# A re-searched instruction order for linear attention with a gated feed-forward layer, with two subtractions moved to VectorE

## The chip, the cores and the metric

The kernel runs on one core of a Trainium2 chip. The metric is the device time of one execution in microseconds, the median of several runs; less is better. The core has a TensorE for matrix products, a VectorE, a ScalarE and a GpSimd for element-wise work, and SP (SyncE), whose queue issues every transfer of this kernel. Each engine works through its own list of instructions in order and waits at an instruction until the semaphores that it names have come.

## The reference

Softmax of q over the features, softmax of k over the sequence, a linear attention without a score matrix, and then a feed-forward layer whose two branches are multiplied:

```python
def _attn_ref(q, k, v):                      # each (8, 8, 576, 64)
    q_s = np.exp(q - np.max(q, axis=-1, keepdims=True))
    q_s = q_s / (np.sum(q_s, axis=-1, keepdims=True) + 1e-09)
    k_s = np.exp(k - np.max(k, axis=2, keepdims=True))
    k_s = k_s / (np.sum(k_s, axis=2, keepdims=True) + 1e-09)
    kv = np.einsum('bhsd,bhse->bhde', k_s, v)
    return np.einsum('bhsd,bhde->bhse', q_s, kv)
...
x = attn_out.transpose(0, 2, 1, 3).reshape(4608, 512)
return (x @ w_a) * (x @ w_b) @ w_out         # d_ff = 1536
```

## The kernel before

The 4,608 tokens are worked through in nine chunks of 512. For each chunk the attention gives x, and x goes through the two weight matrices and the output matrix. All large products are done at single precision by splitting each operand into a high and a low part and adding three products. From the second chunk on the two weight products are written as a seven-product block scheme (Strassen's): groups `kx`, `ky` and `ka` of twelve products of 256 columns each, into three banks; the output product is written in the same way from the fifth chunk on, in half groups of six products into the banks `po0` to `po3`. The weight operands `ws` and the right-hand operands `xo` do not all fit on the chip. They are stored to memory once (`dw`, `dr`) and loaded again and again, 512 KB and 256 KB at a time, into a few rotating buffers. A load can start only when the last product that read its buffer is done, and at most eight loads are under way. The attention for the next chunk is interleaved: `qt` are tiles of queries, of which VectorE takes the maxima (`st`), ScalarE the exponentials with their sums; `kt` and `vt` are keys and values, `pk` their products.

The first chunk is a stage of its own, in which everything is started. It works on four pairs of heads. For each pair g the class `Startup` has a small function: `mc` takes the maximum of the keys, `ek` their exponential, `tr` five transposes on TensorE (`pka`, `pkb`), `cA` and `cD` the copies back, `pk` the product with the values; `qs` takes the maxima of the queries, `qu` subtracts them, `qe` takes the exponential, `qr` its sum, `qn` the reciprocal, `qm` scales by it, `pq` transposes the queries, `qw` copies them, and `px` multiplies them with the pair's key-value product. In the version before, `qu` and `qm` are GpSimd's for all four pairs. `wu` multiplies a tile of ones with itself, nine times ahead of the first transposes and twice between the first and the second lot; nothing reads its result.

What order the engines' lists are in is not left to the code. `ORDER` at the top of the file holds, for each of the five engines, a list of positions which says in what order the instructions, counted as the code records them, are to stand; `in_order` chains them. These lists come out of a search that is not in the file.

Of the kernel before, what the change touches and what calls it, by code (L numbers as in the profile page):

```python
# [7 lines left out]
F32 = mybir.dt.float32  # L8
# [23 lines left out]
        "0-15 20 16-19 21-48 53-59 49-52 60 75-84 61-74 97-100 91-94 85-88 101-102 109-110 103-105 111 "  # L32
        "89-90 112-114 106-108 127-132 95-96 115-120 133-138 171-174 121-123 222-225 175 124-126 139-159 "
        "165 200-209 163 166 164 168 170 160-162 176-181 167 273-276 182-187 169 188-196 210 197-199 216 "
        "227-232 239-241 315-318 233-238 242-247 226 248-260 277-282 211-215 366-369 283-285 264 217-218 "
        "286-288 219-221 289-291 270-271 292-294 267 301-302 268 261 295-300 272 269 309 265 408-411 262 "
        "320-322 319 266 323-325 263 306 326-328 344-353 332-333 312 303 334 394-395 329-331 412 335-343 "
        "370-378 437-446 379-390 459-462 391-393 304 307-308 305 354 310-311 313-314 363-365 360-361 "
        "425-427 413-418 357 428-430 355-356 396 431-433 358 419-424 501-504 405 362 402-403 487-488 "
        "434-436 359 399-400 404 406-407 401 543 529-530 397-398 447 456-458 453-454 568 455 463-471 "  # L40
        "450-452 475-483 472-474 492-494 484-486 448-449 505-510 498-500 489-491 517-522 511-513 534-536 "
        "514-516 523-525 495-497 526-528 537-539 544-546 531-533 547-558 575 629-638 559-564 576-577 "
        "565-567 540-542 581-592 687 578-580 572-574 623-625 569-571 617-622 605-616 626-628 736 639-644 "
        "651-656 645-650 737 657-662 593-604 663-674 738-747 675-686 688-705 748-759 712-723 727-728 "
        "730-731 729 784 775-777 785 732-734 760-765 786 766-771 706-711 735 781-783 797-802 724-726 "
        "803-814 772-773 815-820 832-843 774 844-849 778-780 850-855 871-872 874-875 873 856-861 880-891 "
        "862-867 876 910-911 868-869 877-878 870 879 913-914 787-796 892-903 821 907-908 904-906 916-939 "
        "909 940-957 912 915 958-963 985-986 964-975 982-984 988-993 987 1021 976-977 1022 978 822-831 "
        "979-980 1000-1008 994-999 1009-1011 1018-1020 981 1012-1013 1024-1028 1014 1029 1015-1016 "
        "1042-1053 1030-1041 1072-1083 1096-1097 1023 1017 1105-1106 1099-1100 1107 1098 1101 1060-1065 "  # L50
        "1054-1056 1066-1071 1057-1059 1102-1103 1084-1095 1104 1114-1137 1141-1142 1138-1139 1144-1145 "
        "1147-1148 1146 1156-1161 1168-1179 1162-1167 1149 1108-1111 1143 1140 1112-1113 1180-1191 "
        "1228-1239 1219-1220 1216-1217 1204-1209 1218 1222-1223 1150 1225-1226 1151 1210-1215 1192-1197 "
        "1224 1221 1152-1154 1227 1240-1251 1155 1198-1203 1252-1253 1261-1263 1258-1259 1264-1269 "
        "1255-1256 1270-1275 1257 1276-1287 1254 1260 1372-1391 1288-1299 1336-1347 1312-1323 1333-1335 "
        "1300-1305 1330-1331 1348-1353 1327-1329 1354-1359 1306-1311 1369-1370 1332 1363-1365 1371 "
        "1324-1326 1360-1361 1366-1367 1392-1397 1464 1398-1403 1362 1404-1415 1368 1416-1427 1465-1470 "
        "1428-1445 1452-1453 1446-1451 1471-1476 1458-1459 1455-1456 1477-1482 1457 1483-1488 1461-1463 "
        "1498-1499 1454 1521-1532 1501-1510 1460 1533-1544 1489-1491 1545-1550 1495-1496 1492-1493 "
        "1557-1568 1551-1556 1494 1584-1586 1569-1574 1581-1582 1500 1497 1587-1589 1623-1624 1593-1599 "  # L60
        "1590-1592 1583 1600-1604 1575-1580 1617-1618 1620-1621 1605-1616 1625-1628 1622 1619 1511-1520 "
        "1629-1655 1659-1676 1656-1658 1701-1702 1698-1699 1695-1696 1704-1705 1697 1737-1738 1703 "
        "1677-1682 1706 1746-1747 1683-1694 1707-1718 1700 1740-1741 1719-1724 1742 1725-1736 1743-1744 "
        "1749-1753 1739 1745 1755-1760 1754 1761-1766 1748 1767-1778 1785-1796 1779-1781 1797-1802 "
        "1782-1783 1803-1808 1821-1822 1827-1829 1809-1820 1833-1850 1784 1824-1825 1851-1856 1826 "
        "1860-1861 1823 1857-1858 1863-1864 1830-1832 1866-1867 1859 1862 1865 1868-1910 1941-1952 "
        "1932-1933 1938-1939 1935-1936 2085-2094 1929-1930 1917-1928 1940 1934 1968-1969 1953-1964 1970 "
        "1911-1916 1977-1982 1931 1937 1983-2000 1971-1972 1974-1976 1965-1967 2013-2018 2049-2051 2001 "
        "2052 2019 2053 1973 2043-2044 2002 2020-2021 2003-2006 2022-2024 2007-2011 2040-2041 2046-2048 "
# [1676 lines left out]
```

## Time and profile before

| | us |
|---|---|
| median of three timed runs | 934.03 |
| lowest and highest of them | 933.91, 935.12 |
| the profiled execution | 938.13 |
| its span, first to last instruction | 936.4 |
| TensorE busy | 914.3 (98%) |
| VectorE busy | 714.4 (76%) |
| ScalarE busy | 492.1 (53%) |
| GpSimd busy | 113.6 (12%) |

The mean granted clock of TensorE over the span is 0.995 of full speed. 306.40 MB are moved, at a mean of 327 GB/s. Of the chain of work that ended last, 76% of the span is TensorE's, 11% transfers, 5% VectorE, 4% ScalarE. The engines overlap, so busy shares do not add up; only the idle time of the engine that sets the pace, and the clock at which it works, can be won.

### The profile page before, as it was taken

What the parts mean: (1) busy time and instruction counts of PE and PEld (TensorE: products, weight loads), DVE (VectorE), ACT (ScalarE), POOL (GpSimd) and SP (SyncE); (2) the same over time, 40 slices, a digit from 0 to 9 for tenths busy, and PEclk for the clock granted to TensorE, in tenths of its full rate; (3) what the DMA queues carried; (4) which work ended last, traced back from release to release, by engine and by line L of the source; (5) the groups of instructions that cost most, each with busy time, mean ns of one, the idle gap of its engine ahead of it and who ended that gap; (6) DMA issues with size and microseconds to landing.
All of it is one profiled execution on the core that took longest, in us unless ns stands there. A gap on an engine that the chain in (4) does not pass through costs nothing.

```text
span 936.4 us, 19574 instructions
## 1 busy us (share of the span) xinstructions
PE 914.3 (98%) x7171; PEld 855.8 (91%) x7171; DVE 714.4 (76%) x1554; ACT 492.1 (53%) x1350; POOL 113.6 (12%) x96
## 2 busy tenths in 40 slices
PE   7999999999999999999999989999999999999998
PEld 6667888898898999999999989999999999999997
DVE  5889988587877777679877777588868776776556
ACT  5988787555433446545834653336543554343322
POOL 4545344422000000000000000000000000000000
PEclk8999999999999999999999999999999999999999
DMA  9899999999999999999899888998999799959962
GB/s 356 321 380 398 367 343 359 354 346 331 348 353 321 351 347 313 376 317 377 316 344 334 315 299 293 298 378 288 356 314 392 254 348 307 391 197 321 335 245 108
DMA packets 124735, 306.40 MB, mean 327 GB/s; under 512 B 13408, under 2 KB 30432, under 8 KB 124640
## 3 DMA queue, kind: packets, MB, share of 16 engines
q1 hardware_dynamic: 124640, 305.16, 92.1%
q8 instruction: 57, 0.93, 0.4%
q14 instruction: 38, 0.31, 0.1%
HBM read 256.87 MB, written 48.23 MB: 326 GB/s over the span
## 4 chain that ended last, share of the span: by engine, by line
PE 76%; DMA 11%; DVE 5%; ACT 4%; issue 2%; SPq 1%; POOL 0%; DVEq 0%; ACTq 0%
PE kx L855 24%; PE po L1518 15%; PE ky L855 12%; PE po L884 8%; PE ka L855 6%; PE pt L830 6%; DMA ws<-dw 3%; PE px L786 2%; PE pk L604 2%; DMA kt<-in_k 2%; DMA mr<-dq 2%; DMA qt<-in_q 1%; DMA xo<-dr 1%; ACT qt L697 1%; DMA dw<-ws 1%
## 5 line engine op out<-in xcount | busy, mean ns | idle before, releaser
L855 PE MATMUL kx<-xo,ws 128*128 128x256 f32 x2304 | 316.6, 283 | 1.9 <-ACT u L1621 1.0
L855 PEld LDWEIGHTS kx<-xo,ws 128*128 128x128 f32 x2304 | 293.5, 189 | 9.3 <-ACT u L1621 2.3
L855 PE MATMUL ky<-xo,ws 128*128 128x256 f32 x1152 | 158.4, 282 | 1.2 <-DMA ws<-dw 0.8
L855 PEld LDWEIGHTS ky<-xo,ws 128*128 128x128 f32 x1152 | 146.5, 188 | 3.0 <-PE px L786 0.9
L1472 DVE TENSOR_TENSOR left<-cc,left 128x256 fp32r<-128x256 f32 x245 | 96.6, 421 | 53.3 <-ACT left L1471 52.6
L1471 ACT CAST left<-cc 128x256 fp32r<-128x256 f32 x245 | 92.4, 405 | 71.0 <-DVE cc L1487 36.5
L1518 PE MATMUL po<-xo,left 128*128 128x256 f32 x750 | 106.8, 283 | 1.9 <-DMA xo<-dr 1.9
L1518 PE MATMUL po<-kept,left 128*128 128x256 f32 x720 | 100.5, 282 | 1.6 <-DVE acc L1527 1.6
L1518 PEld LDWEIGHTS po<-xo,left 128*128 128x128 f32 x750 | 97.3, 190 | 2.9 <-issue 1.9
L1518 PEld LDWEIGHTS po<-kept,left 128*128 128x128 f32 x720 | 91.9, 189 | 1.9 <-DVE acc L1527 1.8
L855 PE MATMUL ka<-xo,ws 128*128 128x256 f32 x576 | 81.5, 283 | 2.1 <-DMA ws<-dw 2.1
L830 PE MATMUL pt<-xo,ws 128*128 128x512 f32 x288 | 77.7, 406 | 2.9 <-ACT ga L837 2.2
L697 ACT ACTIVATE qt<-qt,st 128x64 f32<-128x64 f32 x224 | 76.2, 343 | 7.5 <-DVE st L694 6.3
L855 PEld LDWEIGHTS ka<-xo,ws 128*128 128x128 f32 x576 | 74.1, 188 | 3.4 <-issue 1.7
L1621 ACT COPY u<-kx 128x512 f32<-128x512 f32 x48 | 28.2, 587 | 82.3 <-DVE cc L1615 41.2
L830 PEld LDWEIGHTS pt<-xo,ws 128*128 128x128 f32 x288 | 52.8, 189 | 18.5 <-ACT ga L837 3.1
L534 POOL PARTITION_ALL_REDUCE mx<-m x20 | 15.8, 790 | 431.9 <-DVE m L545 431.9
L1487 DVE TENSOR_TENSOR cc<-cc 128x256 f32<-128x256 f32 x140 | 56.9, 420 | 1.8
L884 PE MATMUL po<-wo_w,gh 128*128 128x512 f32 x192 | 56.4, 398 | 0.0
L1642 ACT COPY cc<-kx 128x256 f32<-128x256 f32 x48 | 17.9, 372 | 72.4 <-PE kx L855 72.4
L1602 ACT COPY u<-kx 128x512 f32<-128x512 f32 x48 | 28.1, 585 | 50.1 <-PE kx L855 50.1
L1607 ACT COPY u<-kx 128x512 f32<-128x512 f32 x48 | 28.0, 584 | 48.7 <-PE kx L855 48.3
(173 smaller groups left out, 1376.8 us busy)
## 6 DMA issues: line engine op xcount, KB each, us to landing
ws<-dw SPq DMA_DIRECT2D x277, 512.0 KB, 6.5
xo<-dr SPq DMA_DIRECT2D x125, 256.0 KB, 5.7
dw<-ws SPq DMA_DIRECT2D x42, 512.0 KB, 6.4
mr<-dq SPq DMA_DIRECT2D x112, 128.0 KB, 6.5
raw<-in_w_ab SPq DMA_DIRECT2D x24, 512.0 KB, 7.2
vt<-in_v SPq DMA_DIRECT2D x28, 325.0 KB, 6.3
qt<-in_q SPq DMA_DIRECT2D x32, 256.0 KB, 5.9
kt<-in_k SPq DMA_DIRECT2D x24, 320.0 KB, 5.2
```

The lines of the kernel that those rows point to most:

```text
L604: nc.tensor.matmul(pk[h * D:(h + 1) * D], kt[:, j, h], vt[:, j, h], start=(j == 0), stop=(j == J - 1),)
L697: nc.scalar.activation(out=qt[:, j, h], in_=qt[:, j, h], func=AF.Exp, bias=st[:, h, 0, j:j + 1], accum_out=st[:, h, 1, j:j + 1],)
L830: nc.tensor.matmul(pt, w[:, wp], x[g][:, xp], start=(g == 0 and i == 0), stop=(g == NP - 1 and i == 2),)
L855: ins = nc.tensor.matmul(pt[:, n], w[:, n, wp, c], x[:, xp, c], start=(first and n == 0 and i == 0), stop=(i == 5), skip_group_check=True,)
L884: nc.tensor.matmul(po[t], a[:, ts], wo[f][:, w], start=(f == 0 and i == 0), stop=(f == NF - 1 and i == 2),)
L1471: nc.scalar.copy(out=a[:, 0], in_=cc[:, n, part])
L1472: nc.vector.tensor_tensor(out=a[:, 1], in0=cc[:, n, part], in1=a[:, 0].bitcast(F32), op=ALU.subtract)
L1487: nc.vector.tensor_tensor(out=o, in0=x, in1=y, op=op)
L1518: nc.tensor.matmul(pt[:, t], x.left[:, ap, t * P:(t + 1) * P], w[:, wp], start=(first and t == 0 and n == 0), stop=(n == 2), skip_group_ch ...
L1602: nc.scalar.copy(out=u3, in_=kx)
L1607: nc.scalar.copy(out=u2, in_=kx)
L1621: nc.scalar.copy(out=u4, in_=kx)
```

## The change

Three things are written differently, and the lists for all five engines are new.

```diff
-    whole_q = (nc.gpsimd, nc.gpsimd, nc.gpsimd, nc.gpsimd)
-    WARM = (9, 2)
-    QM = (0, 1, 2, 3)
+    whole_q = (nc.vector, nc.vector, nc.gpsimd, nc.gpsimd)
+    QM = (1, 2, 3)
...
         def wu(n):
-            if n == 0:
-                at["wu"] = ps.tile([P, T], F32, name="wu", tag="po3")
-            for i in range(WARM[n]):
-                nc.tensor.matmul(at["wu"][:, 0:P], ones, ones, start=True, stop=True)
+            wu = ps.tile([P, T], F32, name="wu", tag="po3")
+            for w in (T, T, H):
+                nc.tensor.matmul(
+                    wu[:, 0:w].rearrange("p (n q) -> p n q", q=P), ones,
+                    ones.unsqueeze(1).broadcast_to([P, w // P, P]), start=True, stop=True,
+                )
...
-        "wu0 mc0 qs0 ek0 mc1 qu0 qe0 tr0 wu1 qs1 cD0 qu1 ek1 qr0 qn0 mc2 qe1 tr1 qm0 cA0 ek2 pk0 qr1 "
+        "wu0 mc0 qs0 ek0 mc1 qu0 qe0 tr0 qs1 cD0 qu1 ek1 qr0 qn0 mc2 qe1 tr1 qm0 cA0 ek2 pk0 qr1 "
...
 ORDER = {
     "PE": (
-        "0-15 20 16-19 21-48 53-59 49-52 60 75-84 61-74 97-100 91-94 85-88 101-102 109-110 103-105 111 "
...
+        "0-2 7 3-6 8-36 45 37-40 46 41-44 47-51 53-62 67-76 52 63-66 83-85 89-94 77-79 86 101-102 87-88 "
```

So the subtractions of the first two pairs and the scaling of the first are VectorE's, and GpSimd has three instructions fewer; the eleven products of ones of 128 columns are three of 512, 512 and 256 columns, all ahead of the first transposes. The new lists come from a search that counts a transfer as landing later than the search before did. They hold the same other instructions; line numbers above the change are one lower in the new file, and the numbers at the ends of tile names are eight lower in the late stages.

Three places show how the lists differ. The first is the start on VectorE, before and after (`mc` are maxima of keys, line 1169 the maxima of queries, 1175 the subtraction, 1192 the sum, 1195 and 1196 the reciprocal, 1199 the scaling, `pkb` what the last transpose of a pair wrote):

```order
L1132 TENSOR_REDUCE mc<-kt_first_77 128x1
L1132 TENSOR_REDUCE mc<-kt_first_79 128x1
L1169 TENSOR_REDUCE qst<-qts 128x8 x2
L1150 COPY kt_first_77<-pkb 128x128
L1169 TENSOR_REDUCE qst<-qts 128x8
L1192 TENSOR_REDUCE qst_143<-qts 128x8
L1132 TENSOR_REDUCE mc<-kt_first_81 128x1
L1195 TENSOR_SCALAR qst_143<-qst_143 128x8
L1150 COPY kt_first_79<-pkb 128x128
L1192 TENSOR_REDUCE qst_160<-qts 128x8
L1196 RECIPROCAL qst_143<-qst_143 128x8
```

```order
L1169 TENSOR_REDUCE qst<-qts 128x8
L1175 TENSOR_TENSOR qts<-qts,qst 128x512
L1169 TENSOR_REDUCE qst<-qts 128x8
L1148 COPY kt_first_77<-pkb 128x128
L1148 COPY kt_first_79<-pkb 128x128
L1192 TENSOR_REDUCE qst_137<-qts 128x8
L1175 TENSOR_TENSOR qts<-qts,qst 128x512
L1195 TENSOR_SCALAR qst_137<-qst_137 128x8
L1169 TENSOR_REDUCE qst<-qts 128x8
L1130 TENSOR_REDUCE mc<-kt_first_81 128x1
L1196 RECIPROCAL qst_137<-qst_137 128x8
L1192 TENSOR_REDUCE qst_152<-qts 128x8
```

Two subtractions have come in, both copies out of `pkb` stand ahead of the first sum, and the row that follows the last one shown is the scaling of the first pair (line 1199). On GpSimd the instruction named ISA and the rest of its list follow each other as before, without the three:

```order
L1175 ISA
L1175 TENSOR_TENSOR qts<-qts,qst 128x512
L353 MEMSET mask 64x64
L1175 TENSOR_TENSOR qts<-qts,qst 128x512 x2
L1199 TENSOR_TENSOR qts<-qts,qst_143 128x512
L1199 TENSOR_TENSOR qts<-qts,qst_160 128x512
L389 TENSOR_TENSOR wr<-raw,wr 128x512
```

```order
L1175 ISA
L1175 TENSOR_TENSOR qts<-qts,qst 128x512
L1199 TENSOR_TENSOR qts<-qts,qst_152 128x512
L388 TENSOR_TENSOR wr<-raw,wr 128x512
L1175 TENSOR_TENSOR qts<-qts,qst 128x512
```

The first subtraction and the first scaling in GpSimd's list are now those of the third and the second pair.

The second place is SP's list near 545 us, before and after (`qt` is the fourth tile of queries of the seventh chunk, `ws` are weight operands, `xo` right-hand operands, `kt` keys):

```order
L1456 DMA xo_4423<-dr06_3381 128x512
L498 DMA ws_7305<-dw13_1884 128x1024
L498 DMA ws_7327<-dw11_1901 128x1024
L498 DMA ws_7389<-dw14_482 128x1024
L498 DMA ws_7413<-dw12_2001 128x1024
L668 DMA qt_7259<-in_q 128x512
L1456 DMA xo_4424<-dr04_3374 128x512
L1456 DMA xo_4424<-dr02_3364 128x512
```

```order
L1456 DMA xo_4415<-dr06_3373 128x512
L497 DMA ws_7297<-dw13_1876 128x1024
L667 DMA qt_7251<-in_q 128x512
L497 DMA ws_7319<-dw11_1893 128x1024
L497 DMA ws_7381<-dw14_474 128x1024
L497 DMA ws_7405<-dw12_1993 128x1024
L497 DMA ws_7470<-dw16_557 128x1024
L1456 DMA xo_4416<-dr02_3356 128x512
```

The load of queries has moved ahead of three loads of weights.

The third place is TensorE's list some microseconds later, between the third and the fourth group into one `kx` bank:

```order
L855 MATMUL kx_6992<-xo_6793,ws_6906 128x256 x12
L604 MATMUL pk_7169<-vt_7003,kt_7001 64x65 x10
L604 MATMUL pk_7169<-vt_7007,kt_7005 64x65 x6
L855 MATMUL kx_6992<-xo_6881,ws_6938 128x256 x12
L1518 MATMUL po1_6061<-xo_4423,left_4511 128x256 x6
```

```order
L854 MATMUL kx_6984<-xo_6785,ws_6898 128x256 x12
L1518 MATMUL po0_6045<-kept10_3602,left_4502 128x256 x6
L1518 MATMUL po0_6045<-xo_4416,left_4501 128x256 x6
L603 MATMUL pk_7161<-vt_6995,kt_6993 64x65 x10
L603 MATMUL pk_7161<-vt_6999,kt_6997 64x65 x10
L1518 MATMUL po0_6045<-kept11_3605,left_4506 128x256 x6
L1518 MATMUL po0_6045<-xo_4415,left_4505 128x256 x6
L854 MATMUL kx_6984<-xo_6873,ws_6930 128x256 x12
```

Between the two groups there now stand four half groups of `po` and 20 small products, where there were 16 small products.

## Rows read from the trace of the kernel before

**Rows 1.** The page: TensorE's totals, and the transfer engines' share in 40 slices.

```profile
PE 914.3 (98%) x7171; PEld 855.8 (91%) x7171; DVE 714.4 (76%) x1554; ACT 492.1 (53%) x1350; POOL 113.6 (12%) x96
...
DMA  9899999999999999999899888998999799959962
```

**Rows 2.** Timeline to 40 us: start, length, engine, line, operation, count [idle before, releaser].

```profile
0.98 4.21 PE L1164 MATMUL wu<-ones 128*128 128x128 f32 x18 [0.98 <-POOL ones L348]
...
5.40 0.69 DVE L1169 TENSOR_REDUCE qst<-qts 128x8 f32<-128x512 f32 x1
...
6.04 1.08 PE L1142 MATMUL pka<-ident,kt_first 128*128 128x128 f32 x4 [0.86 <-DMA ident<-in_eye]
...
7.46 0.29 DVE L1150 COPY kt_first<-pkb 128x128 f32<-128x128 f32 x1
...
9.45 1.03 POOL L1175 TENSOR_TENSOR qts<-qts,qst 128x512 f32<-128x512 f32 x1 [8.18 <-issue]
...
10.52 0.63 ACT L1183 ACTIVATE qts<-qts 128x512 f32<-128x512 f32 x1 [2.71 <-POOL qts L1175]
10.52 0.69 DVE L1169 TENSOR_REDUCE qst<-qts 128x8 f32<-128x512 f32 x1 [2.77 <-POOL qts L1175]
...
11.78 0.81 DVE L1132 TENSOR_REDUCE mc<-kt_first 128x1 f32<-128x640 f32 x1
...
12.51 0.16 DVE L1195 TENSOR_SCALAR qst<-qst 128x8 f32<-128x8 f32 x1
...
13.37 0.19 DVE L1196 RECIPROCAL qst<-qst 128x8 f32<-128x8 f32 x1
...
13.71 2.05 POOL L1199 TENSOR_TENSOR qts<-qts,qst 128x512 f32<-128x512 f32 x2 [1.12 <-DVE qst L1195]
...
14.81 2.12 PE L1213 MATMUL pq<-ident,qts 128*128 128x128 f32 x8 [1.41 <-POOL qts L1199]
...
19.71 0.62 PE L1142 MATMUL pka<-ident,kt_first 128*128 128x128 f32 x4
```

**Rows 3.** Windows: stretch, length, busy us (instructions) by engine, granted clock, transfer share, GB/s.

```profile
5.00:10.00 5.00, 4.14 (x35) 3.63 (x34) 2.06 (x4) 1.78 (x3) 0.55 (x1) 1.00 1.01 374
10.00:15.00 5.00, 1.49 (x27) 1.04 (x22) 4.43 (x13) 4.10 (x7) 3.88 (x6) 0.79 1.04 416
15.00:20.00 5.00, 5.00 (x19) 3.58 (x19) 2.65 (x11) 2.67 (x6) 4.04 (x4) 0.53 1.03 405
...
562.00:564.00 2.00, 2.00 (x13) 2.00 (x12) 2.00 (x5) 0.74 (x1) 0.00 (x0) 0.61 0.97 368
```

**Rows 4.** The tile `qt`: VectorE's scaling, duration in ns (least, median, most), starts.

```profile
L684 DVE TENSOR_TENSOR qt<-qt,qst x4: 679/760/1187, 52.2 to 105.2; 128x512 f32<-128x512 f32 x4
```

**Rows 5.** TensorE's waits, by releaser: us in total, times, longest.

```profile
PE ka L855 <- DMA ws<-dw: 2.1, 3, 1.5
...
PE po L1518 <- DMA xo<-dr: 1.9, 4, 0.9
PE po L1518 <- DVE acc L1527: 1.6, 1, 1.6
...
PE ky L855 <- DMA ws<-dw: 0.8, 1, 0.8
```

**Rows 6.** Timelines of SP, ScalarE, VectorE and TensorE near 550 us.

```profile
543.37 5.41 SPq L498 DMA_DIRECT2D ws<-dw  x4
549.11 0.33 SPq L668 DMA_DIRECT2D qt<-in_q  x1
...
544.69 0.58 ACT L1602 COPY u<-kx 128x512 f32<-128x512 f32 x1
...
556.22 0.69 DVE L694 TENSOR_REDUCE st<-qt 128x8 f32<-128x512 f32 x1 [2.24 <-DMA qt<-in_q]
...
561.68 1.04 PE L1518 MATMUL po<-kept,left 128*128 128x256 f32 x6 [1.63 <-DVE acc L1527]
```

**Rows 7.** The chain of waits from 520 us: the first half group at full clock again.

```profile
566.32 0.72 PE po L1518 x6
```

More of the change, by code (lines that the diff above doesn't have):

```diff
@@ L31 @@
     "PE": (
[97 rows of a table removed]
[95 rows of a table added]
     ),
     "Activation": (
[45 rows of a table removed]
[45 rows of a table added]
     ),
     "DVE": (
[68 rows of a table removed]
[68 rows of a table added]
     ),
     "Pool": (
-        "0-1 3-4 2 5 7 6 8-10 13 15 11-12 14 16-19 21-22 20 24-25 23 27 26 28-31 33 32 34-37 39 38 40 42 "
-        "41 43 45-46 44 47-91 "
+        "0-7 10 12 8-9 11 13-16 18 17 19 21-22 24 20 25 23 27 26 28 30 29 31-34 36 35 37 40 39 38 42-43 "
+        "41 44-88 "
     ),
     "SP": (
[33 rows of a table removed]
[34 rows of a table added]
     ),
```

483 rows, old and new, of the table ORDER are left out of this document.

## The prediction

> **What bounds the kernel now.** I read the page's totals first. TensorE is busy for 914.3 of 936.4 us [rows 1], so 22.1 us is all the time in which it stands still, and no reordering can return more than that and what a lowered clock costs. Then I asked where the 22.1 us lie. 0.98 us pass before the first product; the windows show 0.86 us from 5 to 10 us and 3.51 us from 10 to 15 us; in the next window TensorE is busy throughout, but at a mean granted clock of 0.53, which is the 1.2 GHz level nearly all the time [rows 2, 3]. From there on the idle time is thin. The list of TensorE's waits names transfers for 2.1 us (`ka`), 0.8 us (`ky`) and 1.9 us (`po`), and one wait of 1.6 us for VectorE [rows 5]. The last of these is also a transfer, one step removed, and it brings the clock down a second time: from 562 to 564 us the granted clock is 0.61 [rows 3, 6].
>
> So there are two stages to price: the start, where a chain through GpSimd, VectorE and ScalarE sets the time, and the long rest, where TensorE sets it and late transfers make the holes.
>
> **The start.** The subtraction of the first pair runs on GpSimd at 9.45 us, although its maxima were ready at 5.40 + 0.69 = 6.09 us; the trace shows 8.18 us in front of it in which GpSimd waited for nothing else [rows 2]. The order shows an instruction named ISA on that engine just ahead of its first subtraction, before and after. In the new list that subtraction is VectorE's and does not stand behind it. A subtraction or scaling of this shape on VectorE takes 0.68 us [rows 4]. By hand, with the durations of rows 2: maxima done at 6.09, subtraction to 6.8, the exponential on ScalarE (0.63) to 7.5, maxima of the second pair to 7.5. Then VectorE waits in its new order for the last of ten transposes on TensorE, which start at 6.04 and take about 1.08 us for four, so about 8.4 (the two single products of ones between them are gone). What is queued behind that wait is the sum of the first pair and the second pair's subtraction, and both wait with it. The copy (0.29) ends at 8.7, the sum of the first pair (the same tile read as for the maxima, 0.69) at 9.4, the second subtraction at 10.1; then a small addition (0.16), the third pair's maxima (0.69), the third key's maximum (0.81), a reciprocal (0.19), the sum of the second pair (0.69) and the first scaling (0.68) add 3.2 us, some 0.3 us less by overlap: about 13.0. The first transposes of queries began at 14.81 [rows 2], so they are 1.8 us earlier. The second pair's scaling stays on GpSimd: its reciprocal is ready at about 13.5, and half of 2.05 us brings it to 14.6, against 13.71 + 2.05 = 15.76 before. The chain behind both needs the second too, so I take 1.1 us, with ends 0 and 2.4 (1.1, and 1.3 more if the clock comes up one dense stretch sooner, below).
>
> What does this cost VectorE? Three more operations, 2.0 us, all before 13 us, where it had been idle for 2.77 us up to 10.52 us, waiting in its list for GpSimd [rows 2]. That idle stretch is the cover. On SP's queue the keys of the third pair move ahead of its queries, and the fifth raw weight tile moves behind two tiles of `w_out` and one of queries, 1.28 MB; at 405 to 416 GB/s [rows 3] that is 3.1 us later. Four other weight tiles stand ahead of it in ScalarE's list of conversions, and they are the cover, so I cost it at nothing; without that cover it is up to 3.1 us on ScalarE, the whole gain of the start and more.
>
> The price of 0.68 us has an upper end. The four operations of rows 4 took 0.68 us at best and 1.19 us at worst. The Trainium skill (SBUF — State Buffer, Who interferes with whom) says that a VectorE instruction with two SBUF inputs contends with a GpSimd instruction that reads SBUF, and the slow one fits that. By it the moved operations keep the low price only where GpSimd stands still; in my list it does (nothing before 10.8 us, nothing from 11.8 to 13.3 us). If all three met it, the start would lose 3 x 0.51 = 1.5 us and its gain would be gone.
>
> The three products of ones stream 1,280 columns before the transposes, against 1,152 in nine before and 256 in two between. The nine ended at 0.98 + 4.21 = 5.19 us [rows 2]; at the same rate the three end near 5.7, and the transposes cannot start before 5.9, when the identity lands. I cost them at zero.
>
> **The late transfer at 549 us.** One load of queries is issued at 549.11 us and VectorE's maxima over it start at 556.22 us after 2.2 us of waiting [rows 6]. VectorE works in order, so a bank of sums that TensorE wants back is emptied late; TensorE idles 1.63 us, and the four half groups after that run from 561.68 to 566.32 us, 4.64 us for what takes 4 x 0.72 = 2.88 us at full clock [rows 6, 7]. Idle time and clock together: 1.63 + 1.76 = 3.4 us. In the new lists the load stands one place behind the first of four weight loads instead of behind all four, which alone took 5.41 us to issue [rows 6]. Its buffer comes from another tile, released after one exponential that follows ScalarE's copy `u` (544.69 us on the old clock), so near 545.6 us. With the same 7.1 us to land, it is there at 552.7 us. VectorE asks for it earlier too, near 551.4 us, so 1.3 us of its wait stay; but TensorE now has four half groups of `po` and 20 small products between the two `kx` groups that hang on this (some 4.5 us), where before it had 16 small products (1.2 us). I take the 3.4 us as gone, with ends 0 and 3.4.
>
> **The other late transfers.** The waits on `ws` and `xo`, 2.1 + 0.8 + 1.9 = 4.8 us [rows 5], are a matter of how many products stand between the release of a buffer and the first use of what is loaded into it. Followed through the lists, nine `xo` loads have fewer than 56 products' time before, one after; for `ws` the shortest lead stays the same. I take half, 2.4 us, ends 0 and 4.8. A new list also makes new close places; I charge 1.0 us, between 0 and the longest transfer wait of the old one, 1.5 us, twice.
>
> **The sum.** The profiled execution took 938.13 us, 1.73 us around its span; the three timed ones have a median of 934.03 us, 4.1 us less. Late transfers are what differs most easily between executions, so I assume the timed ones hold half of the 8.2 us of late transfers that the profile shows. Profiled: -1.1 - 3.4 - 2.4 + 1.0 = -5.9, about 932.2 us. For the median: -1.1 - 5.8/2 + 1.0 = -3.0, which is 931.0 us.
>
> **The rivals.** *Handed back.* The transfer engines are near full until 20 us [rows 3] and stay so for most of the span [rows 1]; the first load is issued at the same time as before, and the same bytes must come. If the start's gain only lets TensorE reach the weights of 230 us earlier, it waits there for what it gained. The rest of the lists then do not do what they say: one stall goes, another comes, and the time is 933 to 934.5 us, no change. For it: the `ka` waits of 2.1 us are of that stage; for `ws` the leads are no longer than before. Against it: the two largest stalls are elsewhere.
>
> *The clock comes up sooner.* Before, it fell near 12.8 us after the thin stretch from 10 us and rose at 19.7 us, after five dense microseconds [rows 2, 3]. Dense work now starts 1.1 to 1.8 us sooner, and wide products might keep the clock up from the start. Then 1.3 us more come back: 928.5 us with the stalls gone. Against wide products doing so: 4.21 us of ones in a row are followed by transposes at 1.08 us for four, where 0.62 us is the price at full clock [rows 2]. The Trainium skill (TensorE: Matmul & The Clock Gate, Part 1) says that warming up is a matter of time under load and not of how many products are issued; by it three wide ones do no more than nine narrow ones.
>
> *Slower.* At 545 us three weight loads now stand behind the load of queries. Each slot in that list is 5.41 / 4 = 1.35 us where it waits for buffers. If one of them had less cover than a slot, TensorE waits 1.4 us for it, and the clock falls as it did at 562 us, 1.8 us more, after which the next loads, which wait for TensorE's releases, are later too. With the start's gain handed back that is 934.0 + 3.2 = 937 us. It decides where the cover is below 1.35 us. Against it: no `ws` wait shows there before.
>
> **Chances.** Forecast, start kept and about half the stalls gone, 929 to 932.1: 0.42. Clock sooner as well, 927 to 929: 0.10. Handed back, within 0.2%: 0.28. Slower by over 0.2%: 0.20. A measurement of this kernel tells about 0.2%, 1.9 us, from no change, so faster has 0.52. For 8 in 10 the range is 927.0 to 936.6; the likeliest case's own is 929 to 932.1.
>
> **What would show it.** Right: GpSimd's first subtraction is the third pair's; the first query transposes start near 13 us; no wait of TensorE for VectorE near 560 us and no second fall of the clock; fewer than 5 us of TensorE's waits name a transfer. Wrong: the first query transposes begin near 14.8 us as before; the sum of transfer waits is unchanged or larger; the granted clock falls at a new place in the long stage.

## The result, and the profile after

The changed kernel took 918.75 us (median of four runs, 917.89 to 920.35) beside 933.97 for the kernel before: a ratio of 0.9847, 95% interval 0.9813 to 0.9882. Run once more beside other runs of the kernel before, it took 921.25 us (920.18 to 923.41), a ratio of 0.9882, interval 0.9855 to 0.9908. Over all runs the medians are 920.4 us (10 runs) and 932.6 us (83 runs), so the change is worth some 12 us, 1.3%. Three executions of 1,776 to 2,256 us, two of the kernel before and one of `new_from_470` below, are over 1.5% above the fastest of their kernel and in no figure here. I had forecast 931.0 with a range from 927.0. The direction was right and the size about a quarter of what came.

The profiled execution shows 20.2 us less span (916.2 for 936.4), 5 to 8 us more than the timed runs: the profiled execution of before was a late one, as the prediction said. The lines of the page of the changed kernel that answer to [rows 1], and its chain of work that ended last:

```profile
PE 904.6 (99%) x7155; PEld 850.2 (93%) x7155; DVE 714.4 (78%) x1557; ACT 492.5 (54%) x1350; POOL 113.2 (12%) x93
...
PEclk8999999999999999999999999999999999999999
DMA  9999999999999999999999989998999799959962
...
PE 89%; DMA 5%; ACT 2%; DVE 2%; issue 1%; SPq 0%; DVEq 0%; ACTq 0%
```

TensorE's idle time fell from 22.1 to 11.6 us, and its *busy* time fell as well, from 914.3 to 904.6. That second half I had not looked for. The table of windows shows it by stage. The cuts are the moments at which TensorE has done the same work in both kernels (30, 150, 480 and 555 us of products at full rate, with 0.119 us for 256 columns and 0.231 for 512, the medians of the spacing of products in these traces). Each row is a stretch, its length, and the busy time of TensorE, its weight loads, VectorE, ScalarE and GpSimd (instructions in brackets), then the granted clock, the transfer engines' share and GB/s. First the kernel before:

```profile
0.00:52.90 52.90, 46.13 (x263) 32.88 (x264) 38.66 (x82) 41.82 (x88) 26.69 (x28) 0.94 0.91 336
52.90:182.50 129.60, 126.40 (x740) 103.52 (x739) 111.71 (x218) 97.30 (x260) 55.70 (x38) 1.00 1.00 367
182.50:523.60 341.10, 337.37 (x2746) 320.35 (x2745) 262.26 (x572) 167.54 (x462) 26.24 (x24) 1.00 0.98 343
523.60:607.00 83.40, 79.18 (x694) 77.50 (x693) 59.94 (x145) 41.54 (x134) 2.14 (x3) 0.98 0.87 292
607.00:936.30 329.30, 325.23 (x2734) 321.58 (x2733) 241.83 (x540) 143.87 (x410) 2.87 (x4) 1.00 0.86 302
```

and the changed one:

```profile
0.00:50.60 50.60, 43.71 (x247) 29.23 (x248) 41.18 (x85) 42.76 (x94) 24.65 (x25) 0.93 0.98 369
50.60:177.00 126.40, 125.45 (x733) 103.18 (x733) 114.19 (x220) 99.45 (x275) 55.07 (x38) 1.00 1.00 370
177.00:512.10 335.10, 335.10 (x2752) 320.74 (x2751) 259.31 (x571) 166.51 (x454) 27.54 (x24) 1.00 0.99 349
512.10:588.40 76.30, 76.27 (x695) 75.63 (x694) 59.52 (x145) 39.61 (x122) 2.46 (x3) 1.00 0.94 318
588.40:916.20 327.80, 324.03 (x2735) 321.43 (x2733) 240.22 (x538) 144.18 (x409) 3.48 (x4) 1.00 0.87 304
```

Read the third row of each: the same work takes 341.1 us before and 335.1 after. Only 3.7 of the 6.0 us are idle time of TensorE; the other 2.3 us were busy time. Here a wait cost more than its idle time. In the kernel before, one group of 12 products behind a wait:

```profile
230.53 1.66 PE L855 MATMUL ka<-xo,ws 128*128 128x256 f32 x12 [1.50 <-DMA ws<-dw]
```

At full rate twelve of these take 12 x 0.119 = 1.43 us, so this wait cost 1.73 us and shows 1.50. (A group with no wait ahead also lasts 1.59 us from its start to its end, the median of 89 in this stage, but there the first 0.16 us lie under the group before it.) TensorE stands still nine times in this stage, and the four groups of twelve products behind such a wait lasted 1.66 to 1.71 us; at 0.25 us each, nine make 2.2 us, an estimate that comes near the 2.3.

The start, in the timeline of the changed kernel (start, duration, engine; in brackets the idle time ahead), beside [rows 2]:

```profile
0.98 3.87 PE L1161 MATMUL wu<-ones 128*128 128x512 f32 x6 [0.98 <-POOL ones L347]
...
6.20 0.69 DVE L1175 TENSOR_TENSOR qts<-qts,qst 128x512 f32<-128x512 f32 x1
...
6.58 1.04 PE L1140 MATMUL pka<-ident,kt_first 128*128 128x128 f32 x8
...
8.98 0.68 DVE L1175 TENSOR_TENSOR qts<-qts,qst 128x512 f32<-128x512 f32 x1
...
10.48 1.05 POOL L1175 TENSOR_TENSOR qts<-qts,qst 128x512 f32<-128x512 f32 x1 [9.03 <-DVE qst L1169]
...
11.64 0.68 DVE L1199 TENSOR_TENSOR qts<-qts,qst 128x512 f32<-128x512 f32 x1
...
12.42 1.09 PE L1213 MATMUL pq<-ident,qts 128*128 128x128 f32 x4 [0.59 <-issue]
...
12.83 1.04 POOL L1199 TENSOR_TENSOR qts<-qts,qst 128x512 f32<-128x512 f32 x1 [1.31 <-DMA raw<-in_w_ab]
```

The first query transposes stand at 12.42 us; before they stood at 14.81. TensorE's waits over the whole span, longest in total first (us, times, longest):

```profile
PE pk L603 <- DMA vt_first<-in_v: 2.0, 1, 2.0
PE pkb L1140 <- ACT kt_first L1134: 1.6, 1, 1.6
PE wu L1161 <- POOL ones L347: 1.0, 1, 1.0
PE pk L603 <- DVE kt L590: 0.7, 1, 0.7
```

All four lie in the start. Of the waits of [rows 5] one is left in the long stage, 0.2 us for `ws`. All that I had named as signs of being right came true: GpSimd's first subtraction is the third pair's, the query transposes begin at 12.42 us, no wait for VectorE and no fall of the clock are left near 560 us, and TensorE's waits for transfers come to 2.6 us. So these signs say nothing of the size.

### The profile page after: what moved, and what is told of

Read it like the earlier page. It is cut to its first block, busy times and chain, and to the rows that moved or that the text cites. A ratio compares the mean times of both kernels' runs of the same rounds, so it can differ in the third digit from the quotient of the medians.

```text
span 916.2 us, 19531 instructions
## 1 busy us (share of the span) xinstructions
PE 904.6 (99%) x7155; PEld 850.2 (93%) x7155; DVE 714.4 (78%) x1557; ACT 492.5 (54%) x1350; POOL 113.2 (12%) x93
## 4 chain that ended last, share of the span: by engine, by line
PE 89%; DMA 5%; ACT 2%; DVE 2%; issue 1%; SPq 0%; DVEq 0%; ACTq 0%
PE kx L854 30%; PE po L1518 19%; PE ky L854 15%; PE po L883 9%; PE ka L854 8%; PE pt L829 3%; PE px L785 2%; PE pk L603 2%; DMA raw<-in_w_ab 2%; DMA wo_raw<-in_w_out 1%; DMA dw<-ws 1%; DMA kt_first<-in_kt 1%; PE pl L1682 1%; DMA ws<-dw 1%; ACT wr L382 0%
## 5 line engine op out<-in xcount | busy, mean ns | idle before, releaser
L854 PE MATMUL kx<-xo,ws 128*128 128x256 f32 x2304 | 312.4, 282 | 0.0
L1621 ACT COPY u<-kx 128x512 f32<-128x512 f32 x48 | 28.2, 587 | 80.1 <-PE kx L854 39.1
L1607 ACT COPY u<-kx 128x512 f32<-128x512 f32 x48 | 28.1, 586 | 50.5 <-PE kx L854 50.3
L1622 DVE TENSOR_TENSOR cc<-ky,u 128x512 f32<-128x512 f32 x48 | 33.0, 688 | 20.6 <-ACT u L1621 16.7
```

The lines of the kernel that those rows point to most:

```text
L854: ins = nc.tensor.matmul(pt[:, n], w[:, n, wp, c], x[:, xp, c], start=(first and n == 0 and i == 0), stop=(i == 5), skip_group_check=True,)
L1607: nc.scalar.copy(out=u2, in_=kx)
L1621: nc.scalar.copy(out=u4, in_=kx)
L1622: nc.vector.tensor_tensor(out=cc[:, 3], in0=ky, in1=u4, op=ALU.add)
```

## The experiments

The numbers of `ORDER` are positions of instructions as the code records them, so a list of the kernel before can be written in the numbers of the changed code. "Loss" below is the time at which TensorE has done a given amount of work, less that work at full rate, from one profiled execution.

**Which stage: old and new lists joined.** `old_lists` is the changed code under the old lists. The other three follow the new list on each engine up to what had begun by 35, 145 or 470 us, and the old list for what is left.

```diff
  "DVE": (          # old_lists: the old order in the new numbers, with 3, 6 and 11 put in
-   0 2 1 3-5 13 7 6 8 16 10 9 12 11 20 14 21 15 17 22 ...
+   0 2 1 3-5 16 7 6 10 8 13 12 9 11 14 20-21 15 22 17-18 ...
  "SP": (           # new_to_35: 35 transfers in the new order, then the old one
-   25 23 29 40 21 42 41 26 38 35 47 31 54 ...
+   25 23 29 40 21 42 41 26 28 32 47 36 39 ...
  "SP": (           # new_to_145: 145 transfers, likewise
-   121 112 130 126 115 114 135 131 122 132-133 141 ...
+   121 112 130 126 115 114 135 131 132 122 141 ...
  "SP": (           # new_to_470: 454 transfers, likewise
-   441 443 442 431 445 432 446-447 472-473 503 ...
+   441 443 442 431 445 432 472-475 463 447 446 ...
```

> The changed program with the order lists of before: the three wide products and VectorE's three operations are in, the three put at the first place where their input is there, and everything else stands in the old order. Theory A, by the lag of TensorE's products in the two traces (span minus the time that the products done so far need at full rate: 3.4 us of difference up to 35 us, 6 between 150 and 310 us, 7 between 500 and 600 us): these edits can bring only the start's part, so 930 to 933 us against about 934. Theory B, the gain is in the start and what follows from a start that is sooner: 918 to 922. My prediction's start alone: 933.

Measured: 929.59 us, ratio 0.9961 (0.9944 to 0.9978), so 3.6 us less than before, just below what theory A allowed.

> The changed program, in which each engine follows the new list for what had begun by 35 us in its trace, and then the old list for what is left. Theory A (each stage's part comes from that stage's order): the whole of the start's part, 3.4 us by the traces, so 929.5 to 931. Theory B (start, and what follows from it): 918 to 922. Theory C (a sooner start is handed back at the next late transfer): 933 to 934.5.

Measured: 928.83 us, 0.9960 (0.9942 to 0.9978), a little below theory A. In the profiled executions this kernel is 1.8 us ahead of `old_lists` at 30 us of work and level with it at the end of the products (46.48 and 46.51 us of loss). What the new lists add to the start may be handed back under the old lists that follow; but the later stages of one kernel order differ by more than this from execution to execution (table below), so two executions do not show it.

> As the run before, with the new lists for what had begun by 145 us. Theory A: between 35 and 145 us the two traces differ by 0.5 us more, so within 1 us of the run that changes at 35 us, 929 to 931. Theory B: 918 to 922. Theory C: 933 to 934.5.

Measured: 926.83 us, 0.9938 (0.9917 to 0.9959), lower than theory A expected.

> As the run before, with the new lists for what had begun by 470 us. Theory A: 6 us more than at 145 us in the profiled runs, and the part of 500 to 600 us is still missing, so 923 to 926 us, with waits left near 540 us. Theory B: 918 to 922 and no waits near 540 us. Theory C: over 930.

Measured: 924.35 us, 0.9908 (0.9885 to 0.9930), as theory A had it; but its profiled execution, the fastest of the six, shows no wait of TensorE between 512 and 590 us, where theory A expected one.

**The counterpart**, old lists first, new lists for what had not begun by 478 us of `old_lists`:

```diff
  "SP": (           # new_from_470: 452 transfers in the old order, then the new one
-   433 468-470 441-442 472 443 473 431-432 474 ...
+   433 468-470 441-442 472 443 431 445 432 446-447 ...
```

> The changed program with the old lists for what the kernel with the old lists had begun by 478 us (the same place in TensorE's work as 470 us of the changed kernel), and the new lists for what is left: the counterpart of the run that follows the new lists to 470 us. Theory A, each stage's order acts in its own stage: the step from 924.4 to 918.8 that the end's order made there is made here too, so 929.6 - 5.6 = 924 us. Rival: the new order of the end pays only on top of the new order ahead of it (other loads are in flight when it begins), so 928 to 930.

Measured: 928.35 us, 0.9950 (0.9931 to 0.9969): about 1 us from `old_lists`, the rival's number. In its own profile the loss of this stage falls as in the changed kernel (table below), yet the time hardly follows.

**The load of queries at 549 us**, moved alone in the old list, and moved back alone in the new one:

```diff
  "SP": (           # early_q, in the kernel before
-   497 506 522-523 528 530 515 509 507 516
+   497 506 522 515 523 528 530 509 507 516
  "SP": (           # late_q, in the changed kernel
-   506 522 515 523 528 530 533 507
+   506 522-523 528 530 515 533 507
```

> The kernel before with one load moved: the block of Q that arrived at 556.2 us, issued behind four loads of split weights, is issued ahead of the last three of these, as the new lists have it; nothing else. My prediction: 3.4 us (1.63 us of waiting and 1.76 us of half clock). The lag of the traces between 500 and 600 us differs by 7 us: if this one load makes all of that, the time falls by 7; if it is one of several that land late, by 2 to 4; if the weights behind it are then late instead, by 0 or less.

Measured: 935.53 us, 1.0020 (0.9996 to 1.0043): no gain. The load came in time, and VectorE stood at the next late load instead. Its timeline, and what TensorE waited for from 490 to 600 us:

```profile
556.13 0.43 DVE L543 TENSOR_TENSOR m<-kt 128x256 f32<-128x256 f32 x1 [3.13 <-DMA kt<-in_k]
```

```profile
PE po L1518 <- DVE acc L1527: 1.6, 1, 1.6
PE kx L855 <- ACT u L1621: 1.6, 1, 1.6
```

The same addition (`acc`) queues behind another waiting operation, TensorE waits the same 1.6 us as in [rows 6], and the clock falls again in this execution.

> The changed kernel with the same load moved back behind three loads of split weights. If the load's place alone made the fall of the clock near 562 us, it comes back here: 3 to 7 us slower, with idle TensorE and a stretch at half clock near 545 us. If its place was harmful only together with what else landed late in the old order, the time stays within 1 us of the changed kernel's.

Measured: 924.49 us, 0.9911 (0.9886 to 0.9936), 3 to 6 us over the changed kernel. Here one place decides: VectorE waits for this load, and TensorE for VectorE (timeline, then TensorE's waits from 500 to 600 us):

```profile
541.54 0.69 DVE L693 TENSOR_REDUCE st<-qt 128x8 f32<-128x512 f32 x1 [3.92 <-DMA qt<-in_q]
```

```profile
PE po L1518 <- DVE acc L1527: 3.3, 1, 3.3
PE po L1518 <- DMA xo<-dr: 0.8, 1, 0.8
```

**The additions ahead of the waiting operation**, in VectorE's list of the kernel before:

```diff
  "DVE": (          # acc_first
-   951 920 960-961 926-927 957 962 924 937 958
+   951 920 924 937 960-961 926-927 957 962 958
```

> The kernel before with one edit in VectorE's list: the two additions into the sums (L1537, L1527) that stood behind the maximum over the late block of K at 558.3 us stand ahead of it. Moving the late block of Q alone bought nothing: in that run VectorE waited 3.13 us for the block of K instead, and TensorE the same 1.6 us for the same addition. Theory, the additions stand in a queue behind operations that wait for loads, and whichever load is late holds them: TensorE's wait of 1.63 us near 561 us and the fall of the clock at 562.5 us are gone, and the time falls by 2 to 4 us. Rival, TensorE waits for the next late transfer instead: 0, and a wait of the same size within 10 us.

Measured: 932.67 us, 1.0004 (0.9986 to 1.0021). In its profile the wait and the second fall of the clock are gone (TensorE waits 0.7 us in all from 490 to 600 us), and the timed runs do not change. So the stall of [rows 6] belonged to the profiled execution: taking it away buys nothing in the median, to within 1.3 us.

**The parts of the start**, first in the new lists (`narrow_ones`, `pool_sub`), then alone in the kernel before (`dve_in_old`, `wide_in_old`):

```diff
  # narrow_ones: the old products of ones, the rest of the change kept
-  for w in (T, T, H):
+  for i in range(WARM[n]):                 # WARM = (9, 2)
  # pool_sub: GpSimd again
-  whole_q = (nc.vector, nc.vector, nc.gpsimd, nc.gpsimd);  QM = (1, 2, 3)
+  whole_q = (nc.gpsimd, nc.gpsimd, nc.gpsimd, nc.gpsimd);  QM = (0, 1, 2, 3)
  # dve_in_old: the kernel before with VectorE's three operations
-  whole_q = (nc.gpsimd, nc.gpsimd, nc.gpsimd, nc.gpsimd);  QM = (0, 1, 2, 3)
+  whole_q = (nc.vector, nc.vector, nc.gpsimd, nc.gpsimd);  QM = (1, 2, 3)
  # wide_in_old: the kernel before with the three wide products
-  for i in range(WARM[n]):
+  for w in (T, T, H):
```

> The changed kernel with the old products of ones: nine of 128 columns ahead, two behind the first five transposes, all else in the new order. My prediction took the wide ones' part for 0: then the same time within 0.5 us and the transposes near 6.5 us at half clock in both. In the trace of the changed kernel eight transposes near 6.5 us took 1.04 us where four took 1.08 before, that is the full clock: if the wide ones make this, the transposes here take the double again, the clock rises some 5 us later, as before (9.5 us against 4.0), and the time is 1 to 3 us longer.

Measured: 922.58 us, 0.9886 (0.9857 to 0.9916), beside 0.9882 for the repeated changed kernel: no difference.

> The changed kernel with the first two pairs' subtraction and the first scaling back on GpSimd, all else in the new order. My prediction gave VectorE's three operations and the order by hand 1.1 us. If GpSimd's late first operation (it ran from 9.45 us before, 8.18 us after the last thing it had done) holds up the first query transposes again, these stand near 14.8 us rather than 12.4, and the time is 1 to 3 us longer; if something else holds the start, it stays within 0.5 us.

Measured: 922.75 us, 0.9891 (0.9864 to 0.9918). In its profile the first query transposes stand at 15.29 us, late as the first of the two expectations has it, and TensorE has lost 23.45 us by 30 us of work, 3.2 us more than the mean of the kernels with the new start; the time does not show it within its interval.

> The kernel before with VectorE's three operations alone, put where the kernel with the old lists has them; products of ones as before. Together with the wide products they gave 0.9961. If VectorE's operations make it, 929 to 930.5; if the wide products do, 932 to 934.

Measured: 930.16 us, 0.9970 (0.9949 to 0.9990): VectorE's operations, 2.8 us.

> The kernel before with the three wide products of ones in the place of the eleven narrow ones, all else as before. My prediction: 0, so 932 to 934. If the clock that they bring up makes the gain of the two edits, 929 to 930.5.

Measured: 932.18 us, 0.9998 (0.9977 to 1.0020): the wide products, nothing, as forecast. And this although in its profile the clock was up at the first transposes. Whether it is up there does not go with the width of the products. Four lines from the timelines of `narrow_ones`, `late_q` (wide), `wide_in_old` and `dve_in_old` (narrow):

```profile
6.10 0.60 PE L1141 MATMUL pka<-ident,kt_first 128*128 128x128 f32 x4
```

```profile
6.56 1.92 PE L1140 MATMUL pka<-ident,kt_first 128*128 128x128 f32 x8
```

```profile
6.45 0.63 PE L1141 MATMUL pka<-ident,kt_first 128*128 128x128 f32 x4 [0.84 <-ACT kt_first L1135]
```

```profile
5.82 1.09 PE L1142 MATMUL pka<-ident,kt_first 128*128 128x128 f32 x4 [0.63 <-DMA ident<-in_eye]
```

Four transposes take about 0.6 us at one level of the clock and about 1.1 at the other; narrow and wide products each stand ahead of both.

**The changed kernel again, and a try to better it** with two more wide products in TensorE's wait at 7.7 us:

```diff
-  for w in (T, T, H):
+  for w in ((T, T, H), (T, T))[n]:
-  "... qe0 tr0 qs1 cD0 ..."
+  "... qe0 tr0 wu1 qs1 cD0 ..."
   "PE": (
-   0-2 7 3-6 8-12 13-36 ...
+   0-2 7 3-6 10-14 8-9 15-38 ...
```

> The changed kernel once more, beside the runs that it is compared with: 917.9 to 920.4, as measured; if those four runs were luck, 921 to 924, and the kernels with one part taken back (922.6 and 922.8) would not differ from it.

Measured: 921.25 us, 0.9882 (0.9855 to 0.9908). The first four runs were on the lucky side, and the two kernels of 922.6 and 922.8 do not differ from this.

> The changed kernel with two more products of ones, 512 columns wide, in the 2.02 us that TensorE waits for the first block of V at 7.7 us (they take 1.7 us at full clock). If the fall of the clock at 10.8 us comes from that wait, it does not fall there, and what TensorE does between 10.8 and 17.6 us at half clock takes 2 to 3 us less, 916 to 917 us; if VectorE and ScalarE set the pace there, or the wait for the block of V grows into the products, the same time within 1 us.

Measured: 920.15 us, 0.9872 (0.9843 to 0.9900): the same. The clock comes back sooner, but the products themselves ran at half clock (3.53 us where I had planned 1.7) and stand ahead of the next ones (timeline, then two windows; the column behind the engines is the granted clock):

```profile
8.52 3.53 PE L1163 MATMUL wu<-ones 128*128 128x512 f32 x4
11.98 1.39 PE L603 MATMUL pk<-vt_first,kt_first 128*64 128x65 f32 x40
13.82 0.63 PE L1215 MATMUL pq<-ident,qts 128*128 128x128 f32 x4 [0.45 <-issue]
```

```profile
10.00:15.00 5.00, 4.00 (x47) 2.00 (x45) 5.00 (x15) 2.94 (x5) 1.81 (x2) 0.82 1.05 417
15.00:20.00 5.00, 4.68 (x58) 3.43 (x58) 4.63 (x14) 4.90 (x10) 3.97 (x4) 1.00 1.03 408
```

In the changed kernel the clock was 0.58 and 0.74 in these windows; its loss at 30 us of work was 20.64 us, here 20.53.

**What the lists repair.** The loss by stage of all kernels whose stage is whole, one profiled execution each (in brackets how many), says how much of a stage's part is order and how much one execution's chance:

```
work done, us     old order of that stage          new order               mean difference
   0 to  30       22.9 to 23.3, mean 23.1 (4)      19.2 to 20.9, 20.3 (8)      -2.8
  30 to 150        9.6 to 11.1, mean 10.3 (8)       5.7 to  9.6,  7.3 (8)      -3.0
 150 to 480        7.2 to 11.8, mean  9.9 (9)       5.1 to  7.1,  6.0 (7)      -3.9
 480 to 555        1.8 to  8.4, mean  3.9 (9)       1.0 to  1.7,  1.2 (6)      -2.7
 555 to the end    2.5 to  4.8, mean  3.3 (9)       2.0 to  3.3,  2.5 (7)      -0.8
```

The sum is -13.2 us, beside 12 by the medians. Single values carry the chance of their execution: those of the kernel before and of `dve_in_old` were 5.5 and 6.4 us above their medians, that of `new_to_470` 4.1 us below. In the first row the old order is that of the old code; the old order with the new code (three kernels) gives 21.0 to 22.8. The two columns overlap in the second row, by 0.05 us, and in the last; in the third they come within 0.1 us (the 7.2 is `new_to_145`, which comes to its stage with a new order ahead of it), and in the fourth too. In the fourth row the kernel before has the highest of nine values. `late_q`, which has one place of the old order there, is left out; it lost 6.95.

In the third stage another number goes along with the loss: VectorE's waits for transfers, 11 to 16 us in nine executions with the old order and 2 to 6 in seven with the new. Those of the kernel before:

```profile
DVE qtt L747 <- DMA mr<-dq: 4.3, 2, 3.8
...
DVE m L543 <- DMA kt<-in_k: 3.7, 3, 2.3
DVE y L1425 <- DMA dr<-xo: 3.3, 1, 3.3
...
DVE t L1431 <- DMA dr<-xo: 2.4, 1, 2.4
```

and all of the changed kernel's:

```profile
DVE m L542 <- DMA kt<-in_k: 1.9, 2, 1.5
...
DVE qtt L746 <- DMA mr<-dq: 0.3, 1, 0.3
```

That suggested a cheap repair: the loads that VectorE stands at, moved a few places in SyncE's list, and nothing else.

```diff
  # q_early, kernel before, transfers 90 to 560 of "SP": 75 loads of Q, K, V earlier, 9 by 4 places, 40 by 3, 24 by 2, 2 by 1
-  ... 500 496-497 506 522-523 528 530 515 509 507 516-517 533-534 546 ...
+  ... 500 496-497 506 522-523 515 528 530 516-517 509 507 533-534 518-519 ...
  # q_late4, changed kernel: 76 loads of the same kinds 4 places later
-  ... 506 522 515 523 528 530 533 507 516 518 ...
+  ... 506 522-523 528 530 533 515 507 509 513 ...
```

> The kernel before with 75 of the 76 loads of Q, K and V that stand between the 90th and the 560th transfer of SyncE's list moved four places earlier (Q) or three (the others), two in one case; nothing else is moved. Theory, what the old order loses is VectorE standing at an operation whose load has not landed: its waits for transfers between 182 and 524 us fall from 11 to 16 us to 2 to 6 as with the new lists, and the time falls by 3 to 6 us. Rival, the weights and products behind them in the queue land late instead: VectorE's waits fall, the time does not, 931 to 936.

Measured: 983.27 us, 1.0565 (1.0528 to 1.0602), 51 us longer. Theory and rival both miss it by far. The waits of SyncE's queue and then of TensorE, over the whole span:

```profile
SPq L522 <- PE pk L604: 48.3, 11, 9.9
SPq L668 <- ACT qt L697: 33.4, 11, 8.0
```

```profile
PE ka L855 <- DMA ws<-dw: 16.5, 6, 6.8
PE kx L855 <- DMA ws<-dw: 7.6, 7, 1.9
```

The loads of K and Q now reach the head of SyncE's queue before the tile that they overwrite is free (L522 waited 18.4 us before, now 48.3), and every load of weights behind them waits too. TensorE's wait for `ws` at `ka` rises from 2.1 to 16.5 us.

> The changed kernel with the same 76 kinds of loads moved four places later. Theory: VectorE's waits for transfers between 177 and 512 us rise from 2 to 6 us to over 10, and the time rises by 3 to 8 us over 919 to 921 (one load moved by three places gave 924.5). Rival: the place of these loads matters at one point alone, so that the time is 924 to 925, as with that one load.

Measured: 1001.22 us, 1.0751 (1.0719 to 1.0783), 69 us over the kernel before and 80 us over the changed one. VectorE stands at the late loads, whole span:

```profile
DVE st L692 <- DMA qt<-in_q: 40.8, 10, 7.4
DVE m L541 <- DMA kt<-in_k: 34.2, 11, 6.8
```

and TensorE behind VectorE:

```profile
PE po L1517 <- DVE acc L1526: 8.7, 2, 5.2
PE po L1517 <- DVE left L1471: 8.1, 3, 4.4
```

So these loads, moved together, have a narrow place: one to four places sooner they block the queue, four later they block VectorE. That does not hold for every single load: `early_q` moved one three places sooner and the time stayed. What the new lists add is not these loads moved forward as a whole; that a choice of them makes it is not excluded.

## Why the prediction was wrong, step by step

**VectorE's operations: right in each time, short in what they bring.** By hand I had the first subtraction end at 6.8 us, the second at 10.1, the scaling at 13.0, the first query transposes at 13.0 and the second pair's scaling end at 14.6. The changed kernel shows 6.89, 9.66, 12.32, 12.42 and 13.87; under the old lists `dve_in_old` shows 13.09 and 14.66 for the two sets of transposes. The low price of 0.68 us held (GpSimd stood still at all three, so the upper end of 1.19 us was not met), and VectorE is busy for 714.4 us as before. I priced this at 1.1 us; under the old lists it brought 2.8 alone (interval 0.9 to 4.8, which holds 1.1) and 3.6 with the wide products (2.1 to 5.2, which does not). The three profiles of the new code with the old order of the start have lost 21.0 to 22.8 us at 30 us of work, for 22.93 in the kernel before; that is 0.1 to 1.9 us, and 1.1 lies in it. Whether the rest comes later, one execution each does not tell. Under the new lists the operations bring nothing that the runs tell from zero (`pool_sub`, 0.9891 beside 0.9882).

**The wide products: zero, right.** Wide products in the place of narrow ones gave 0.9998 (0.9977 to 1.0020). The Trainium skill (TensorE: Matmul & The Clock Gate, Part 1) says that a warm-up goes by time and not by the number of products. What the runs show agrees in the one half: fewer and wider products left the time as it was, and by the four lines above the level at the first transposes goes with neither width; that it goes by time no run here shows. My argument from the 1.08 us of [rows 2] rested on one execution, so that it came out right is in part luck: behind the same nine products `acc_first` shows 0.63. The rival that a clock up sooner gives 1.3 us has no support (in `fill2` it comes up sooner and the time is the same), but the intervals are too wide to exclude it.

**The late transfer at 549 us: real in the trace, not in the median.** I priced it at 3.4 us and halved it for the timed runs. `acc_first` took the stall away and gave 0; `early_q` moved the load and gave a stall behind the next load. As a stage, though, 480 to 555 us is 2.7 us better on average, since with the new order it loses 1.0 to 1.7 us, and with the old one 1.8 to 8.4, the kernel before most. Halving one stall came near that by luck. The step was wrong in kind: I named the load, and the rest of VectorE's queue was as late.

**The other late transfers: the term that failed.** I took TensorE's waits that name a transfer, 4.8 us, took half of it, then half again for the timed runs, and set 1.0 us of new close places against it: about 0.2 us of gain. Measured for the stages from 30 to 480 us: 3.0 + 3.9 = 6.9 us. Three things were wrong in it.

The base was too small, and of the wrong kind. I summed only the waits that name a transfer. The longest line of the same list names ScalarE, and [rows 5] left it out:

```profile
PE pt L830 <- ACT ga L837: 2.2, 2, 1.1
```

It lies at 69 and 91 us, stands with 0.9 to 2.2 us in all eight profiles that have the old order from 30 to 150 us of work, and in none of the eight with the new one. Taken over the profiles of the table, TensorE's waits from 30 to 480 us of work are shorter by 4.7 us with the new order: 1.6 us name a transfer, 3.1 us ScalarE or VectorE. The other 2.2 of the 6.9 us show no idle time; a wait cost more than that (busy time fell by 2.3 us between 182 and 524 us). How much of the 3.1 us goes back to a late transfer, one step removed, is not shown: VectorE waited 16 us for transfers from 182 to 524 us, where TensorE waited 2.8, but before that, from 53 to 182 us, only 0.8.

The halving was wrong: single stalls come and go between executions, but their sum by stage does not, and so the old order loses 7.2 to 11.8 us from 150 to 480 us of work in nine of nine, the new one 5.1 to 7.1 in seven of seven.

And the 1.0 us for new close places had no row behind it. On the mean no stage shows such a place; in one execution there is one, in `after_again`, which lost 9.6 us from 30 to 150 us of work with 2.3 us of waits of `kx` for VectorE.

**"No reordering can return more than that", 22.1 us, "and what a lowered clock costs": wrong as a bound.** What came lies below it, but busy time at full clock fell too, as the third row of the windows shows. Against full rate the kernel before loses 59.6 us of its span, the changed one 39.5. That was the number to start from.

**Handed back (0.28 in my chances)** may be what the start alone does under the old lists: `new_to_35` is 1.8 us ahead at 30 us of work and, in that one execution, no faster at the end; its median is 0.8 us below that of `old_lists`, which decides nothing. What I had not weighed is that the same lists which gain the start also loosen what follows. **Slower** needed a load of weights that becomes late behind the load of queries; there was none, and `late_q` shows that the load of queries is the one that could not have stood later.

**What stays open.** The share of the lists is measured (0.9961 to 0.9882 or 0.9847, some 7 to 11 us), and where it lies. Which of the many moved places make it is not: VectorE's shorter waits for transfers go along with it from 150 to 480 us of work, but the two kernels that moved only its loads were 51 and 80 us slower, so that they are the cause is not shown. From 30 to 150 us VectorE hardly waits for transfers in either order (0 to 2.2 us), and the wait of `pt` for ScalarE that is gone there was not tried alone; nor was the list of one engine.

## What to carry to other kernels

Before pricing a reorder, work out what the bounding engine loses against its full rate, stage by stage, from the spacing of its instructions; idle time was the smaller part of it here, and every wait of the bounding engine belongs to the sum, whichever engine it names. Stalls seen in one execution are samples: a single one may be chance, but a stage that loses in every execution is not, so compare several profiles of near-identical kernels before halving or dropping a term. And a load moved forward in the queue is no free insurance: where its buffer was not free yet, as in `q_early`, it held up everything behind it.

## What the runs showed of the hardware

The granted clock of the first 20 us changes from execution to execution with the same program ahead of it. `acc_first`, which starts as the kernel before does, has four transposes at 5.92 us in 0.63 us, the kernel before 1.08 [rows 2], and the kernels in whose profile the clock was up sooner (`wide_in_old`, `fill2`) are no faster in the median (0.9998, and 0.9872 beside 0.9882).

GpSimd's first operation of two tensors began at 9.45 to 10.5 us in all six kernels that gave it the first subtraction, though its input was ready by 7 us and the profile shows no wait in front of it; moving two subtractions and a scaling off that engine gave 2.8 us under the old lists, and nothing that shows under the new ones.

Loads a few places off cost far more than I would have said: 75 loads moved forward by one to four places in a list of 838 cost 51 us, and one load moved back by three places 3 to 6 us.
